# Order of the scale total, two conversions and six loads at the head of the joint down projection

## The chip, the cores and the metric

The kernel runs on one core of a Trainium2 chip. The metric is device time in microseconds (us). The core has a matrix engine (TensorE, "PE" in the profile; its weight loads are "PEld"), three engines for elementwise work (VectorE "DVE", ScalarE "ACT", GpSimd "POOL") and SyncE ("SP"), which in this kernel issues most DMA transfers. Each engine takes its own list of instructions in order; engines wait for each other by semaphores.

## The reference

One transformer block on a sequence of 2048 rows of 1024 values, bf16 in and out: a layer norm and a sliding, dilated attention with an output product (`wo`), added to the input; then a second layer norm and a gated bilinear feed-forward, also added:

```python
g = jnp.einsum("bsd,df->bsf", x, w_gate)      # 1024 -> 3584
u = jnp.einsum("bsd,df->bsf", x, w_up)
h = g * u
return jnp.einsum("bsf,fd->bsd", h, w_down)   # 3584 -> 1024
```

The change lies in the last product, the down projection, for the first two of four chunks of 512 rows.

## The kernel before

The rows are worked in four chunks of 512. Attention is elementwise work on DVE; projections are 128x512 matmuls on PE. The order of the work is written by hand, engine by engine: what is recorded first on an engine runs first on it. The attention of a chunk is a generator, and `pull(n)` records its next n steps at the place where it stands; around the change a step of chunk 3's attention is one DVE instruction on 128x4096 values (L523, L532 or L534, 2.3 us each).

**The joint down projection.** The gated rows h of chunks 0 and 1 are multiplied with `w_down` together, as a 2x2 block product with seven instead of eight block products. A1x are gated rows of chunk 0, A2x of chunk 1 (x: 1 for even, 2 for odd blocks of 128 inner values); B11, B21 are the left 512 columns of `w_down` for even and odd blocks, B12, B22 the right ones. Chunk 0's gated rows stay in on-chip memory. Chunk 1's were written to the DRAM tensor `hd1` (L752) and are loaded back as `a21` and `a22` (`load_h1`, L973 to L979), each in two parts: 8 blocks and 6 blocks. `b12` is loaded by `load_down` (L927) into two tiles. All of these loads are issued by SP.

Where sums of blocks are formed, the operands are converted to f16 in place, with a power of two as scale: `scale_h1` for h, `scale_d` for `w_down`. A scale comes from a sum of absolute values: ACT adds up pieces of the matrix into columns of `l1d` (L635), `rows()` reduces the columns to one value for each partition and casts it to bf16 (DVE, L639 and L640), `total()` adds over the partitions with one matmul with ones on PE (L645) and turns the total into the scale and its inverse with five small DVE instructions (L647 to L654).

The work around the change, in the order in which it is written:

1. `wo_adds(2, ...)`: the `wo` product of chunk 2 on PE, its sums on DVE (L1000), some attention steps between them, and on ACT the absolute sums of B11 and B21 (`abs_blocks`, the last columns that `scale_d` needs).
2. The loop of L1069: four products A11 x B11 into `ex0` to `ex3`, 14 matmuls each (`dprod`, L944). Between them, by `q`, stand the conversions of `a21` and `a22` (`conv_h1`; part 0 on DVE, L925, part 1 on ACT, L923), the half sums S1 = a21 + a22 (`s1_half`, DVE, L1042), `scale_d.rows()` and, after the third product, `scale_d.total()` into the bank of `ey3`.
3. `seed` (ACT, L1067) copies each `ex` times `scale_d` to `ey`; then ACT multiplies `ey` by the scale of h (L1089).
4. A12 x B21 on top of the same `ex` (L1098). Its first matmul overwrites `ex0`, so it waits for `seed(0)`. On DVE beside it: `put` (L784, the finished left half of chunk 0's result), conversions of `b11` and `b12` (L925), and the differences T1 = b12 - b11 in two halves (`t_half`, L937).
5. S1 x T1 into `ev` (L1116), 56 matmuls. The first needs S1 and the first half of T1, the eighth the second half of T1. Then `ey` takes two more products (L1132 and following). On ACT from step 3 on: the conversions of chunk 0's rows (L1095, 14 of 128x512), of `b22` (L1096), and of A12 (L1104).

The tiles of `b22` lie where a22's two parts lay, so their loads wait for the two half sums. `b22`'s loads are the next that SP issues after the six loads above.

Of the kernel before, what the change touches and what calls it, by code (L numbers as in the profile page):

```python
# [78 lines left out]
def kernel(  # L79
# [11 lines left out]
    nc = tc.nc  # L91
# [565 lines left out]
    scale_gu, scale_d, scale_h = Scale("gu", 28), Scale("d", 23), Scale("h", 56)  # L657
# [260 lines left out]
    def f16(ap):  # L918
        return ap.bitcast(F16)

    def to_f16(dst, src, sc, eng=nc.vector):
        if eng is nc.scalar:
            nc.scalar.activation(dst, src, ACTF.Copy, scale=sc)  # L923
        else:
            eng.tensor_scalar(dst, src, sc, None, ALU.mult)  # L925

    def load_down(homes, e, hf):  # L927
        for a, t in enumerate(homes):
            nc.sync.dma_start(t[:, 0:NH, :], wd_e[e][:, bass.ts(a, NH), bass.ts(hf, 512)])
# [12 lines left out]
    def dprod(ps, q, lhs, rhs, fresh, lo=0, n=TC):  # L942
        for k in range(NP):
            nc.tensor.matmul(ps[:, bass.ds(lo, n)], lhsT=lhs[k][:, bass.ts(q, 128)], rhs=rhs[k][:, bass.ds(lo, n)],  # L944
                             start=(fresh and k == 0), stop=(k == NP - 1), skip_group_check=not fresh)
# [13 lines left out]
    def pull(n):  # L959
        for _ in range(n):  # L960
            next(atts[3], None)
# [3 lines left out]
    def halves(parts, name):  # L965
        return [pool.tile([128, KO, TC], BF, tag=tag, name=f"{name}{i}") for i, (pool, tag) in enumerate(parts)]

    b12 = halves(((att, "qD"), (att, "kD")), "b12")
    load_down(b12, 0, 1)
    a21 = halves(((lnTp, "lnT"), (lnTp, "lnT")), "a21")  # L970
    a22 = halves(((lnTp, "lnT"), (wpool, "w")), "a22")

    def load_h1(dst, e, parts=(0, 1)):  # L973
        for i in parts:
            t, k, n = ((dst[0], 0, 8), (dst[1], 8, 6))[i]
            nc.sync.dma_start(t[:, 0:n, :], hd1[:, 2 * k + e:2 * (k + n):2, :])

    load_h1(a21, 0)
    load_h1(a22, 1)  # L979
    state["live"] += 1  # L980

    def cells_of(homes, n=8):
        return [t[:, k, :] for t in homes for k in range(n)][0:NP]
# [55 lines left out]
    def s1_half(i):  # L1039
        n = (8, 6)[i]  # L1040
        s, t = (f16(a[i][:, 0:n, :]) for a in (a21, a22))
        nc.vector.tensor_tensor(s, s, t, ALU.add)  # L1042

    def conv_h1(a, i, eng=nc.vector):
        n = (8, 6)[i]
        to_f16(f16(a[i][:, 0:n, :]), a[i][:, 0:n, :], scale_h1.s, eng)
# [19 lines left out]
    def seed(q):  # L1066
        nc.scalar.activation(ys[q][:], xs[q][:], ACTF.Copy, scale=scale_d.s)  # L1067

    for q in range(4):  # L1069
        dprod(xs[q], q, A11, cells_of(b11, NH), True)  # L1070
        if q == 0:
            conv_h1(a21, 0)
            conv_h1(a22, 0)
            s1_half(0)
            scale_d.rows()
        if q == 1:
            pull(1)
            conv_h1(a21, 1, nc.scalar)
            conv_h1(a22, 1, nc.scalar)
        if q == 2:  # L1080
            scale_d.total(ys[3])
            inv1 = const.tile([128, 1], F32, name="inv_h1d")
            nc.vector.tensor_tensor(inv1[:], scale_h1.inv, scale_d.inv, ALU.mult)
            inv1 = inv1[:]
            for i in range(3):
                seed(i)
    seed(3)
    for q in range(4):
        nc.scalar.activation(ys[q][:], ys[q][:], ACTF.Copy, scale=scale_h1.s)  # L1089
    pull(1)  # L1090
    s1_half(1)
    b22 = halves(((lnTp, "lnT"), (wpool, "w")), "b22")
# [48 lines left out]
    a22 = halves(((att, "vD"), (att, "oD")), "a22r")  # L1141
# [212 lines left out]
```

## Time and profile before

| what | value |
|---|---|
| median of 4 runs | 773.78 us (773.57 to 775.03) |
| the profiled execution | 773.83 us, of which its span, from first to last instruction, is 772.0 us |
| PE busy | 760.2 us, 98% of the span |
| DVE busy | 606.0 us, 78% |
| ACT busy | 513.3 us, 66% |
| POOL busy | 142.1 us, 18% |
| from 412 to 428 us: PE, DVE, ACT busy | 13.37, 14.10, 13.49 of 16 us |
| from 428 to 440 us: PE, DVE, ACT busy | 11.92, 11.80, 12.00 of 12 us |
| granted TensorE clock | 1.000 |

How to read it: a matmul of 128x512 is listed with 379 ns, but matmuls are pipelined, and a new one starts about every 0.216 us; so PE counts as busy for 98% of the span, and what stands still on it is best seen as a gap between starts. In a row of the timeline the numbers ahead are the start in the span and the duration; brackets at the end hold how long the engine had been idle before and what ended that. Instructions of one kind in a row are merged (x14).

### The profile page before, as it was taken

The numbers are of one execution on the slowest core, as the hardware profiler recorded it, in microseconds if no ns is written. First come the engines' busy times: TensorE is split into PE (matmuls) and PEld (weight loads), VectorE is DVE, ScalarE is ACT, GpSimd is POOL, SyncE is SP. The second block draws the span as 40 slices with busy tenths as digits, with TensorE's granted clock in tenths as the row PEclk, the third lists the DMA queues.
The fourth block names the chain that finished last, engine by engine and source line by source line (L and its number), as shares of the span: only waits on it lengthen the run. The fifth ranks groups of instructions, "written<-read, shape, count | busy, mean of one in ns | idle before, by whom it ended". The sixth has DMA issues, their size and how long they took to land.

```text
span 772.0 us, 10243 instructions
## 1 busy us (share of the span) xinstructions
PE 760.2 (98%) x3607; PEld 350.6 (45%) x3663; DVE 606.0 (78%) x718; ACT 513.3 (66%) x979; POOL 142.1 (18%) x152
## 2 busy tenths in 40 slices
PE   8999999999999999999998999999999999999998
PEld 5444444444444444444443444444444444444444
DVE  5629999999999999999999996985553444568863
ACT  4648966423687398778899985836677677788240
POOL 0000000200002000020000001008778687600000
PEclk9999999999999999999999999999999999999999
DMA  7999796999966799479568457674332423740001
GB/s 267 268 256 258 206 273 153 271 312 284 306 206 215 225 293 300 155 263 314 186 202 281 125 189 241 141 178 106 99 102 62 110 63 102 243 139 28 0 28 54
DMA packets 190915, 144.85 MB, mean 188 GB/s; under 512 B 81808, under 2 KB 181136, under 8 KB 188688
## 3 DMA queue, kind: packets, MB, share of 16 engines
q1 hardware_dynamic: 180416, 116.94, 54.0%
q0 software_dynamic: 3584, 22.02, 8.4%
q10 hardware_dynamic: 6864, 5.24, 2.5%
q8 instruction: 28, 0.46, 0.3%
q14 instruction: 23, 0.19, 0.1%
HBM read 110.10 MB, written 27.26 MB: 178 GB/s over the span
## 4 chain that ended last, share of the span: by engine, by line
PE 73%; DVE 16%; ACT 4%; DMA 4%; issue 3%; ACTq 0%; SPq 0%; DVEq 0%
PE ps L431 19%; PE dx L944 6%; PE pz L826 6%; PE py L826 6%; PE px L826 6%; PE pg L431 4%; PE pu L431 4%; PE pv L826 3%; PE ez L944 3%; PE ey L944 3%; DVE pv L523 3%; PE dy L944 3%; DVE prod L477 2%; PE wo L602 2%; PE wo L998 2%
## 5 line engine op out<-in xcount | busy, mean ns | idle before, releaser
L431 PE MATMUL ps<-lnT,w_qkv 128*128 128x512 bf16 x720 | 158.8, 379 | 1.2 <-DMA lnT<-ln 0.4
L431 PEld LDWEIGHTS <-w_qkv 128*128 128x128 bf16 x736 | 71.8, 98 | 86.8 <-issue 0.9
L344 ACT CAST sg<-ps 128x512 bf16<-128x512 f32 x96 | 55.2, 586 | 47.4 <-PE ps L431 38.5
L477 DVE TENSOR_TENSOR prod<-qD,kD 128x4096 bf16<-128x4096 bf16 x32 | 72.2, 2284 | 12.7 <-DMA kD<-kd 12.6
L523 DVE TENSOR_TENSOR pv<-vD,at 128x4096 bf16<-128x4096 bf16 x32 | 72.4, 2285 | 0.2
L826 PEld LDWEIGHTS <-sw 128*128 128x128 f16 x448 | 43.8, 98 | 52.9 <-issue 0.2
L431 PEld LDWEIGHTS <-w_wu 128*128 128x128 bf16 x448 | 43.9, 98 | 52.8
L431 PEld LDWEIGHTS <-w_wg 128*128 128x128 bf16 x448 | 43.8, 98 | 52.9
L826 PE MATMUL px<-lnT,ws 128*128 128x512 bf16 x212 | 53.1, 379 | 0.6
L536 POOL DMA_DIRECT2D od<-oD x4 | 2.2, 542 | 275.6 <-DVE oD L534 275.6
L431 PE MATMUL pwu<-lnT,w_wu 128*128 128x512 bf16 x219 | 52.5, 379 | 0.3
L431 PE MATMUL pwg<-lnT,w_wg 128*128 128x512 bf16 x220 | 52.5, 379 | 0.2
L431 PE MATMUL pg<-lnT,w_wg 128*128 128x512 bf16 x222 | 52.6, 379 | 0.1
L431 PE MATMUL pu<-lnT,w_wu 128*128 128x512 bf16 x218 | 52.4, 379 | 0.3
L826 PEld LDWEIGHTS <-ws 128*128 128x128 f16 x336 | 32.9, 98 | 39.7
L807 POOL TENSOR_TENSOR sw<-ws 128x512 f16<-128x512 f16 x26 | 30.0, 1152 | 85.6 <-PE pv L826 51.9
L944 PEld LDWEIGHTS <-gs 128*128 128x128 f16 (+1 forms) x280 | 27.4, 98 | 36.0 <-issue 3.2
L479 DVE TENSOR_TENSOR prod<-prod 128x4096 bf16<-128x4096 bf16 x16 | 36.6, 2289 | 0.4
L843 ACT COPY py<-px 128x512 f32<-128x512 f32 x28 | 16.0, 570 | 27.5 <-PE px L826 27.5
L808 POOL TENSOR_TENSOR sw<-sw,ws 128x512 f16<-128x512 f16 x26 | 30.0, 1154 | 2.0
L809 POOL TENSOR_TENSOR sw<-ws 128x512 f16<-128x512 f16 x26 | 30.0, 1153 | 0.0
L810 POOL TENSOR_TENSOR sw<-ws,sw 128x512 f16<-128x512 f16 x26 | 30.0, 1153 | 0.0
(334 smaller groups left out, 1471.9 us busy)
## 6 DMA issues: line engine op xcount, KB each, us to landing
w_wg<-in_B_w_gate_dram SPq DMA_DIRECT2D x14, 1024.0 KB, 7.0
w_wu<-in_B_w_up_dram SPq DMA_DIRECT2D x14, 1024.0 KB, 6.4
w_pair<-in_B_w_gate_dram SPq DMA_DIRECT2D x14, 512.0 KB, 4.0
w_pair<-in_B_w_up_dram SPq DMA_DIRECT2D x14, 512.0 KB, 5.3
w_wo<-in_A_wo_dram SPq DMA_DIRECT2D x6, 1024.0 KB, 7.9
w_qkv<-in_A_wqkv_dram SPq DMA_DIRECT2D x5, 1024.0 KB, 11.4
kd<-sg SPq DMA_DIRECT2D x32, 144.0 KB, 4.5
kD<-kd POOLq DMA_DIRECT2D x4, 1152.0 KB, 8.7
```

Of the source, the lines that this page charges most:

```text
L344: nc.scalar.copy(sg[:, HB:HB + TC], ps[:])
L431: nc.tensor.matmul(ps[:], lhsT=wt[:, ko, bass.ts(j, 128)], rhs=rhs[:, ko, :], start=(ko == 0), stop=(ko == KO - 1))
L477: nc.vector.tensor_tensor(prod[:, j], qD[:], kD[:, :, o:o + SUB], ALU.mult)
L479: nc.vector.tensor_tensor(prod[:, :, 0:16], prod[:, :, 0:16], prod[:, :, 16:32], ALU.add)
L523: nc.vector.tensor_tensor(pv[:, j], vD[:, :, o:o + SUB], at[:, w, None, :].to_broadcast((128, DH, SUB)), ALU.mult)
L807: eng.tensor_tensor(sw[:, i, 0], a21, a22, ALU.add)
L808: eng.tensor_tensor(sw[:, i, 1], sw[:, i, 0], a11, ALU.subtract)
L809: eng.tensor_tensor(sw[:, i, 2], a11, a21, ALU.subtract)
L810: eng.tensor_tensor(sw[:, i, 3], a12, sw[:, i, 1], ALU.subtract)
L826: nc.tensor.matmul(ps[:], lhsT=lhs[:, ko, :], rhs=rhs[:, ko, :], start=(fresh and ko == 0), stop=(ko == 3), skip_group_check=not fresh)
L843: nc.scalar.copy(yb[i][:], xb[i][:])
L944: nc.tensor.matmul(ps[:, bass.ds(lo, n)], lhsT=lhs[k][:, bass.ts(q, 128)], rhs=rhs[k][:, bass.ds(lo, n)], start=(fresh and k == 0), stop=( ...
```

## The change

Three things move; no instruction is added or taken away. The loads of `a21` and `a22` are issued ahead of those of `b12`. `scale_d.rows()` stands between the two DVE conversions instead of after the first half sum. Behind `scale_d.total()` now come, on DVE, the first half sum and one attention step, which stood ahead of it; and on ACT the conversion of a22's second part comes after the seeds and the four scalings, where it had come before the seeds.

```diff
@@ -966,7 +966,6 @@
     b12 = halves(((att, "qD"), (att, "kD")), "b12")
-    load_down(b12, 0, 1)
     a21 = halves(((lnTp, "lnT"), (lnTp, "lnT")), "a21")
     a22 = halves(((lnTp, "lnT"), (wpool, "w")), "a22")
@@ -977,6 +976,7 @@
     load_h1(a21, 0)
     load_h1(a22, 1)
+    load_down(b12, 0, 1)
     state["live"] += 1
@@ -1070,23 +1070,23 @@
         dprod(xs[q], q, A11, cells_of(b11, NH), True)
         if q == 0:
             conv_h1(a21, 0)
+            scale_d.rows()
             conv_h1(a22, 0)
-            s1_half(0)
-            scale_d.rows()
         if q == 1:
-            pull(1)
             conv_h1(a21, 1, nc.scalar)
-            conv_h1(a22, 1, nc.scalar)
         if q == 2:
             scale_d.total(ys[3])
             inv1 = const.tile([128, 1], F32, name="inv_h1d")
             nc.vector.tensor_tensor(inv1[:], scale_h1.inv, scale_d.inv, ALU.mult)
             inv1 = inv1[:]
+            s1_half(0)
+            pull(1)
             for i in range(3):
                 seed(i)
     seed(3)
     for q in range(4):
         nc.scalar.activation(ys[q][:], ys[q][:], ACTF.Copy, scale=scale_h1.s)
+    conv_h1(a22, 1, nc.scalar)
     pull(1)
     s1_half(1)
     b22 = halves(((lnTp, "lnT"), (wpool, "w")), "b22")
```

## The prediction

> **What bounds the kernel now.** I read the page's first part, then the waits of PE, then the timeline from 396 to 452 us, engine by engine.
>
> ```profile
> PE 760.2 (98%) x3607; PEld 350.6 (45%) x3663; DVE 606.0 (78%) x718; ACT 513.3 (66%) x979; POOL 142.1 (18%) x152
> ```
>
> PE is the bound over the whole span, so the change can only gain where PE stands still near it. The waits of PE (total, times, longest) show where:
>
> ```profile
> PE ey L645 <- DVE rowbd L640: 2.4, 1, 2.4
> ...
> PE ex L944 <- ACT ey L1067: 0.2, 1, 0.2
> ```
>
> The matmul of `scale_d.total()` is PE's longest wait anywhere. The timeline of the place:
>
> ```profile
> 412.80 9.23 PE L944 MATMUL ex<-w_dn,gs 128*128 128x512 bf16 x41
> ...
> 419.02 0.19 ACT L635 ACTIVATION_READ_ACCUMULATOR junkb<-w_dn 128x1 f32 x1
> 419.12 2.84 ACT L923 ACTIVATE a<-a,sbh 128x3072 f16<-128x3072 bf16 x1
> 420.50 1.28 DVE L925 TENSOR_SCALAR a<-a,sbh 128x4096 f16<-128x4096 bf16 x1 [1.69 <-DMA a<-hd]
> ...
> 421.82 2.29 DVE L1042 TENSOR_TENSOR a<-a,a 128x4096 f16<-128x4096 f16 x1
> ...
> 424.44 0.38 PE L645 MATMUL ey<-rowbd,ones 128*128 128x512 bf16 x1 [2.42 <-DVE rowbd L640]
> ...
> 427.32 2.40 ACT L1067 ACTIVATE ey<-ex,sbd 128x512 f32<-128x512 f32 x4 [1.79 <-DVE ibd L654]
> ...
> 428.03 12.25 PE L944 MATMUL ex<-w_dn,gs 128*128 128x512 bf16 x55 [0.19 <-ACT ey L1067]
> ...
> 429.60 1.75 DVE L1042 TENSOR_TENSOR a<-a,a 128x3072 f16<-128x3072 f16 x1
> ...
> 431.26 0.68 DVE L784 SCALAR_TENSOR_TENSOR h<-ex,h 128x512 bf16<-128x512 f32 x1
> ...
> 434.27 0.69 DVE L784 SCALAR_TENSOR_TENSOR h<-ex,h 128x512 bf16<-128x512 f32 x1 [0.20 <-PE ex L944]
> ...
> 437.00 2.02 DVE L937 TENSOR_TENSOR w_dn<-b,w_dn 128x3584 f16<-128x3584 f16 x1
> ...
> 439.54 2.01 DVE L937 TENSOR_TENSOR w_dn<-b,w_dn 128x3584 f16<-128x3584 f16 x1
> ...
> 440.11 12.25 PE L944 MATMUL ev<-w_dn,a 128*128 128x512 f16 x56
> ```
>
> The reader is to see two things. First the stall: DVE waits for a DMA until 420.50, so the half sum and `rows()` are late and PE waits. Second, what comes after: the second half of T1 ends at 439.54 + 2.01 = 441.55, and the eighth `ev` matmul, which needs it, is due at 440.11 + 7 x 0.216 = 441.62. DVE is 0.07 us ahead of PE there. So PE can start `ev` earlier only if DVE finishes T1 earlier.
>
> **The change part by part.** A matmul's slot is (452.20 - 440.11) / 56 = 0.216 us, from the starts of `ev` and of `ey` after it.
>
> *PE's stall goes.* The absolute sums on ACT end at 419.02 + 0.19 = 419.21. DVE has by then converted a21's first part (start 417.53, next start about 1.2 us on) and runs the reduce and the cast (0.38 us by their rows): the row sums stand at 419.6. PE's 42 matmuls from 412.80 end at 412.80 + 42 x 0.216 = 421.87; the total starts there, not at 424.44, without a wait. The fourth `ex` product starts at 422.09 and A12 x B21 could start 14 slots later, at 425.11.
>
> *The total's tail.* The matmul ends at 421.87 + 0.38 = 422.25. DVE's hand-off from PE costs 0.03 us (ex1's last matmul ends at 434.24, `put` starts at 434.27), so the copy starts at 422.28. Before, copy to first seed took 427.32 - 426.51 = 0.81: seeds start at 423.09. DVE meanwhile has nothing to do from about 420.9 to 422.28: it was behind PE before, and now it waits for PE. Nothing is gained on DVE by the earlier conversion.
>
> *DVE, by itself.* The tail with inv1 takes 427.39 - 426.51 = 0.88, to 423.16. Then the half sum (421.82 to 424.03: 2.21), L534 (2.20) and L523 (429.60 - 427.39 = 2.21): the second half sum could start at 429.78, against 429.60 before.
>
> *ACT, where the conversion was moved.* The seeds and scalings take 0.572 each (2.29 for four). Three seeds run from 423.09 to 424.81. The fourth needs the fourth product, whose last matmul ends at 422.09 + 13 x 0.216 + 0.38 = 425.28; it runs from 425.31 to 425.88, the four scalings to 428.17, and the conversion of a22's second part (2.85 by two rows) to 431.02. Before, it was done at 425.52. Queued behind it on ACT are the 14 conversions of L1095, which start at 431.0 instead of 431.89, so nobody there is late. But the second half sum on DVE waits for it: from 429.78 to 431.05, 1.27 us of a wait which was not there. Behind that wait on DVE stand `put`, four conversions and both halves of T1.
>
> *T1 and PE.* The half sum takes 431.26 - 429.60 = 1.66, so the first `put` starts at 432.71, 1.45 later than before. The second `put` no longer waits for PE: before, it could have started at 432.93 + 1.06 = 433.99 and started at 434.27. That gives 0.28 back. Both halves of T1 are therefore 1.17 later: the second ends at 442.72. PE reaches the end of A12 x B21 at 425.11 + 56 x 0.216 = 437.2, waits about 3.0 us for the first half of T1 (439.02 + 1.17 = 440.19), runs seven matmuls and waits again, about 1.0 us, until 442.75. The other 49 matmuls end at 453.33, against 452.20: **1.1 us later than before**. PE's stall of 2.57 + 0.35 us (425.11 against 428.03) is not gone; it is moved behind A12 x B21 and made longer.
>
> *After it.* From 452.2 to 490 PE is busy 37.70 of 37.8 us and from 490 to 515 24.98 of 25, so there is no idle time in which the 1.1 us could vanish; I pass it to the end. DVE's next work for PE (the sums of L1112, then t2) ended at 450.7 for matmuls due from 452.2 on; both move by the same 1.1, so the spare 1.5 us stays.
>
> *The loads.* SP issues the six loads between 403.49 and 414.6 and then nothing until 424.14, so no other entry is passed. The four `a` loads now have 1.84 MB less ahead of them, 5.3 us at the 349 GB/s of that stretch. Bounds for a22's first part: no gain at all (420.48) or the whole 5.3 us (415.2). At the late end its conversion finishes at 421.8, still ahead of the copy at 422.28; a22's second part (422.6 at the latest) is wanted at 428.17. `b12` lands with the last bytes, about 422.7, and is wanted at 434.1. So the reorder is worth nothing, covered on the one side by DVE's wait for PE's total and on the other by 11 us. Without the cover it would cost DVE what the data is late.
>
> *b22.* Its two loads wait for the half sums and move from 424.14 to about 425.4 and from 431.4 to 432.8. They took 4.9 to 7.1 us, so the second lands by 439.9 at the latest; ACT wants the tiles at 439.6 and 442.8. Behind them SP issues the results' stores and chunk 3's rows, not wanted before the next `wo` at 476. Nothing.
>
> **Bounds of what the trace doesn't show.** The wait of the second half sum for ACT is new. At the low end ACT is done in time and DVE alone decides: the first `put` at 429.78 + 1.66 = 431.44, less 0.28, shift -0.1 us, time 773.7. At the high end the PE to DVE and DVE to ACT hand-offs cost 0.2 us more each than the 0.03 and 0.10 of their rows, and the shift is 1.5. I take 1.1, because each term of it has a row of the same instruction. The other unknown is how PE runs after standing still for 3.0 us; the longest wait in the trace is 2.42, and the granted clock stays 1.00 from 421 to 425 around it. The nearest row of a slow PE is the start of the kernel:
>
> ```profile
> 1.20 4.28 PE L338 MATMUL warm_ps<-warm 128*128 128x512 bf16 x13 [1.20 <-DVE warm L324]
> ```
>
> Thirteen matmuls at full pace take 12 x 0.216 + 0.38 = 2.97 us; these took 4.28. So a slow restart costs between nothing and 1.3 us; I take nothing, by the 2.42 us row.
>
> [...]
>
> **Sum.** The profiled execution took 773.83 us, 0.05 over the median of 773.78: 773.83 + 1.13 = 774.96, say 775.0.
>
> **The rivals.**
>
> *The stall is simply gone: 770.9.* PE keeps 2.92 us if nothing else holds `ev`. For it: the wait for L640 is PE's longest, and it does go. Against: T1 would have to be done 2.9 us earlier, and its DVE chain is the same work without gaps, starting from a copy that PE allows at 422.28.
>
> *DVE does not wait for ACT: 773.7.* The low end above. It needs the moved conversion done by 429.78, 1.2 us ahead of my sum; the fourth seed, which PE releases, speaks against it.
>
> *The gap behind A12 x B21 slows PE: 776.3.* One mechanism: while PE waits about 3.0 us for the first half of T1, its clock drops, and the 1.3 us of the start's row are added to my 1.1. It decides from some length between 2.42 us, which did no harm, and what the new gap turns out to be.
>
> **How the numbers follow.** My forecast (ACT's conversion holds DVE, DVE holds `ev`) gets 0.74. The DVE-only case gets 0.10, the slow restart 0.11, the full gain 0.05. About what a measurement of this kernel can tell from no change is 0.2%, 1.55 us: above 775.4 counts as slower, below 772.3 as faster. Of my forecast's 0.74 I put 0.13 above 775.4, since the high end of the shift touches it; so slower gets 0.11 + 0.13 = 0.24, faster 0.05, within 0.71. The range from 773.6 to 776.4 takes in the low end of the shift, the forecast and the slow restart, and leaves out the full gain.
>
> **What would show it.** The wait of PE at L645 is gone and the total starts near 421.9. The second half sum has an idle time of about 1.3 us ahead of it, ended by ACT L923. The first `ev` matmul shows a wait for DVE L937 of about 2.9 us, a second follows seven matmuls later, and `ey` starts near 453.3. I am wrong if `ev` starts before 440, if the half sum waits for a DMA, or if matmuls after the gap run at a longer slot.

## The result, and the profile after

The changed kernel takes 775.2 us in the median of 41 runs (774.39 to 777.48), the kernel before 774.6 us in 61 runs taken beside it (773.39 to 776.86). The ratio is 1.001, with a 95% interval of 1.0006 to 1.0015: 0.5 to 1.2 us slower. The profiled execution took 775.12 us, with a span of 773.3 us and a mean granted clock of 0.998.

The waits of PE in the changed kernel (total, times, longest): the wait for the row sums (L640) is gone, and one of 2.9 us stands ahead of `ev`.

```profile
PE ev L944 <- DVE w_dn L937: 2.9, 1, 2.9
PE warm_ps L338 <- DVE warm L324: 1.2, 1, 1.2
```

The timeline of the changed kernel, the rows that answer to those of before:

```profile
412.26 9.23 PE L944 MATMUL ex<-w_dn,gs 128*128 128x512 bf16 x41
...
421.33 0.38 PE L645 MATMUL ey<-rowbd,ones 128*128 128x512 bf16 x1
...
421.74 0.16 DVE L647 COPY totd<-ey 128x1 f32<-128x1 f32 x1 [1.46 <-PE ey L645]
...
422.56 1.82 ACT L1067 ACTIVATE ey<-ex,sbd 128x512 f32<-128x512 f32 x3 [1.14 <-DVE ibd L654]
...
427.63 2.88 ACT L923 ACTIVATE a<-a,sbh 128x3072 f16<-128x3072 bf16 x1
...
430.54 1.76 DVE L1042 TENSOR_TENSOR a<-a,a 128x3072 f16<-128x3072 f16 x1 [1.09 <-ACT a L923]
...
437.66 2.02 DVE L937 TENSOR_TENSOR w_dn<-b,w_dn 128x3584 f16<-128x3584 f16 x1
...
439.73 13.93 PE L944 MATMUL ev<-w_dn,a 128*128 128x512 f16 x56 [2.92 <-DVE w_dn L937]
...
440.20 2.01 DVE L937 TENSOR_TENSOR w_dn<-b,w_dn 128x3584 f16<-128x3584 f16 x1
...
453.50 6.85 PE L944 MATMUL ey<-t,gs 128*128 128x512 f16 x31
```

The total's matmul no longer waits, DVE now waits 1.46 us for it, ACT converts a22's second part from 427.63, the second half sum waits 1.09 us for that, T1's halves end at 439.68 and 442.21, and `ev` starts with the first. The 56 `ev` matmuls then take 453.50 - 439.73 = 13.77 us, where before took 12.09. The busy times by stretch of the changed kernel (busy us and counts of PE, PEld, DVE, ACT, POOL, then the granted clock, the DMA share and GB/s) show why:

```profile
430.00:437.00 7.00, 6.81 (x32) 2.98 (x31) 6.46 (x7) 7.00 (x12) 0.00 (x0) 1.00 0.45 154
437.00:440.50 3.50, 0.77 (x3) 0.32 (x3) 3.50 (x4) 3.50 (x5) 0.00 (x0) 0.95 0.09 30
440.50:443.00 2.50, 2.50 (x7) 0.91 (x6) 2.50 (x3) 2.50 (x2) 0.00 (x0) 0.50 0.20 59
443.00:447.00 4.00, 4.00 (x18) 1.73 (x17) 4.00 (x13) 4.00 (x4) 0.00 (x0) 0.93 0.72 227
```

PE is "busy" for all of 440.5 to 443, but with 7 matmuls where 12 fit at 0.216 us each: the granted clock is 0.50.

### The profile page after: what moved, and what is told of

Read it like the earlier page. It is cut to its first block, busy times and chain, and to the rows that moved or that the text cites. A ratio compares the mean times of both kernels' runs of the same rounds, so it can differ in the third digit from the quotient of the medians.

```text
span 773.3 us, 10245 instructions
## 1 busy us (share of the span) xinstructions
PE 762.8 (99%) x3607; PEld 351.4 (45%) x3663; DVE 606.3 (78%) x718; ACT 513.1 (66%) x979; POOL 142.0 (18%) x152
## 4 chain that ended last, share of the span: by engine, by line
PE 95%; DVE 3%; ACT 1%; issue 1%; DVEq 0%
PE ps L431 20%; PE dx L944 6%; PE pz L826 6%; PE pg L431 6%; PE py L826 6%; PE pwg L431 6%; PE pwu L431 6%; PE pu L431 6%; PE px L826 6%; PE wo L998 4%; PE pv L826 3%; PE ez L944 3%; PE ey L944 3%; PE dy L944 3%; PE ev L944 2%; PE wo L602 2%
## 5 line engine op out<-in xcount | busy, mean ns | idle before, releaser
L431 PE MATMUL ps<-lnT,w_qkv 128*128 128x512 bf16 x720 | 158.7, 379 | 0.8
L431 PEld LDWEIGHTS <-w_qkv 128*128 128x128 bf16 x736 | 71.8, 98 | 86.2 <-issue 0.3
L431 PEld LDWEIGHTS <-w_wg 128*128 128x128 bf16 x448 | 43.9, 98 | 52.8
L431 PEld LDWEIGHTS <-w_wu 128*128 128x128 bf16 x448 | 43.8, 98 | 52.9
L431 PE MATMUL pg<-lnT,w_wg 128*128 128x512 bf16 x222 | 52.6, 379 | 0.1
L431 PE MATMUL pu<-lnT,w_wu 128*128 128x512 bf16 x218 | 52.4, 379 | 0.3
L431 PE MATMUL pwg<-lnT,w_wg 128*128 128x512 bf16 x220 | 52.5, 379 | 0.2
L431 PE MATMUL pwu<-lnT,w_wu 128*128 128x512 bf16 x219 | 52.5, 379 | 0.3
```

Of the source, the lines that this page charges most:

```text
L431: nc.tensor.matmul(ps[:], lhsT=wt[:, ko, bass.ts(j, 128)], rhs=rhs[:, ko, :], start=(ko == 0), stop=(ko == KO - 1))
```

## The experiments

Theory A: `ev` starts when T1 is done; T1 is the end of a chain on DVE which in the kernel before starts with the arrival of a22, and in the changed kernel is held by ACT's conversion of a22's second part; behind PE's wait of 2.92 us the clock drops to 0.50. The rivals stand with each run. Ratios are to the kernel before, run beside on the same chip.

**1. ACT's conversion back ahead of the seeds** (the changed kernel, this part undone):

```diff
             conv_h1(a21, 1, nc.scalar)
+            conv_h1(a22, 1, nc.scalar)
...
-    conv_h1(a22, 1, nc.scalar)
     pull(1)
```

> The changed kernel with one part undone: ACT converts a22's second part before the seeds again. Theory A (the moved conversion holds the second half sum, and through it T1 and ev): the conversion ends at about 424.8, the first seed a little later than in the changed kernel (about 424.8 against 423.1), A12 x B21 starts at about 425.5; the second half sum starts when DVE is free, about 429.8, without a wait for ACT; ev starts at about 439.0 after a gap of some 1.4 us, at full clock; time about 773.7 to 773.9, that is 0.1 to 0.2 below before's undisturbed profile (773.83), 1.1 to 1.4 below the changed kernel. Rival B (only the slow clock behind the gap costs anything, and the place of the conversion does not matter): the gap stays near 2.9 us, and the time stays at about 775.

Measured: 773.5 us, ratio 0.9987 (0.9979 to 0.9996). DVE's wait for the total, its second half sum and PE in its timeline:

```profile
421.79 0.16 DVE L647 COPY totd<-ey 128x1 f32<-128x1 f32 x1 [1.46 <-PE ey L645]
...
429.41 1.75 DVE L1042 TENSOR_TENSOR a<-a,a 128x3072 f16<-128x3072 f16 x1
```

```profile
438.60 1.67 PE L944 MATMUL ev<-w_dn,a 128*128 128x512 f16 x7 [1.55 <-DVE w_dn L937]
441.13 10.73 PE L944 MATMUL ev<-w_dn,a 128*128 128x512 f16 x49 [0.86 <-DVE w_dn L937]
```

The half sum starts without a wait, 1.1 us earlier, and so does `ev`, which now shows both waits, one for each half of T1. From the first `ex` matmul to `ey` PE takes 39.39 us, as in before's profile (39.40): PE's old stall has moved, not gone. All 11 executions kept the full clock. Rival B is out: the conversion's place is worth 1.15 us between executions at full clock (spans of 772.75 and 771.6), and the clock the smaller rest of the 1.7 us between the medians.

**2. The loads alone** (the kernel before, with the loads of `a21` and `a22` first):

```diff
-    load_down(b12, 0, 1)
...
     load_h1(a22, 1)
+    load_down(b12, 0, 1)
```

> The kernel before with one part of the change alone: the loads of a21 and a22 ahead of those of b12. Theory A (DVE's chain from a22's arrival to T1 sets ev): DVE's wait of 1.7 us for the load goes, the row sums stand at about 422.6 instead of 424.4, the total's matmul starts at about 422.7, the seeds at about 425.6, A12 x B21 at about 426.3, T1's second half ends at about 439.8, and ev starts at about 438.3 instead of 440.11: 1.8 us less than before, about 772.1. Rival C (what the prediction said of the reorder: it is worth nothing): 773.8. Rival D (the store of the last gated rows holds the first a loads and delays b12 behind them): slower than 774.5.

Measured: 771.82 us, ratio 0.9967 (0.9955 to 0.9979), 5 executions. DVE and PE in its timeline:

```profile
416.81 2.47 DVE L925 TENSOR_SCALAR a<-a,sbh 128x4096 f16<-128x4096 bf16 x2
419.32 2.29 DVE L1042 TENSOR_TENSOR a<-a,a 128x4096 f16<-128x4096 f16 x1
```

```profile
421.94 0.38 PE L645 MATMUL ey<-rowbd,ones 128*128 128x512 bf16 x1 [0.64 <-DVE rowbd L640]
...
437.61 12.25 PE L944 MATMUL ev<-w_dn,a 128*128 128x512 f16 x56
```

This one part, alone, gains what the whole change loses and more. DVE goes from the first conversion to the second without a wait, the first half sum, the seeds and T1 come 2.5 us earlier in the span, PE's wait falls from 2.42 to 0.64, and `ev` follows A12 x B21 without one. C and D are out: the reorder has a value, which the other moves hide. Experiment 1 shows where the first part of it goes. It has the early loads too, with the row sums early and the first half sum and an attention step behind the total, and its median span at full clock is 1.9 us longer (771.6 against 769.7): there DVE stands still 1.46 us for the total's matmul, where here it works on the half sum and an attention step.

**3. Filling the gap** (the changed kernel, with 11 matmuls in it):

```diff
+        for _ in range(11 if q == 0 else 0):
+            nc.tensor.matmul(ev[:], lhsT=ones[:], rhs=scale_d.rowb[:].to_broadcast((128, TC)), start=True, stop=True)
         dprod(ev, q, FS1, fcells(b11), True)
```

> The changed kernel with 11 additional matmuls of ones times the row sums into the bank of ev0, between A12 x B21 and ev, whose results are overwritten; they fill about 2.4 us of the gap of 2.9 us. Theory A (ev's start is set by T1, and the clock drops in the gap): ev's first matmul starts where it did, about 439.7, but at full clock; it now waits again before the eighth, until T1's second half at 442.2, and the next product starts at about 452.9 instead of 453.5: 0.6 to 0.7 us less than the changed kernel in executions where its clock dropped, about 774.4. Rival B (only the clock costs anything): the time falls to that of before or below, 773.8 or less. Rival E (additional matmuls only push ev back): 775 or more.

Measured: 774.54 us, ratio 1.0 (0.9991 to 1.0008), all 12 executions at a clock of 1.0. PE in its timeline:

```profile
436.65 2.56 PE L1117 MATMUL ev<-rowbd,ones 128*128 128x512 bf16 x11
439.73 1.67 PE L944 MATMUL ev<-w_dn,a 128*128 128x512 f16 x7 [0.52 <-DVE w_dn L937]
442.26 10.74 PE L944 MATMUL ev<-w_dn,a 128*128 128x512 f16 x49 [0.86 <-DVE w_dn L937]
452.84 7.50 PE L944 MATMUL ey<-t,gs 128*128 128x512 f16 x34
```

`ev` starts at 439.73, to the digit as in the changed kernel, since T1 does. At full clock it waits again for the second half, and `ey` starts 0.66 earlier (452.84 against 453.50). So the clock costs the changed kernel 0.66 us and not 1.68: its slow matmuls ran where PE would have waited. B and E are out.

**4. Two attention steps behind T1 and t2** (the kernel of experiment 1, with them moved; the five steps are these two, the two that stood there and one more, which had stood among the later sums):

```diff
             s1_half(0)
-            pull(1)
             for i in range(3):
...
-    pull(1)
     s1_half(1)
...
-    pull(2)
+    pull(5)
     retire(4)
```

> The changed kernel with ACT's conversion of a22's second part ahead of the seeds and with the two attention steps of chunk 3 (4.4 us of DVE) behind T1, F11's sums and t2, where now five steps stand instead of two. Theory A (T1's chain on DVE is the bound): the second half sum starts at about 425.4, the puts follow PE (about 428.7, 431.7), T1's halves end at about 436.4 and 439.0, A12 x B21 starts at about 425.5 and ends at 437.6, and ev starts there without a wait: 2.5 us less than before, about 771.3, if the later attention output does not hold chunk 3's wo product (its transposed load lands at about 472 and the product starts at about 473.9). Rival F (that load is late): ev starts as said, but wo waits, and the time is 772 to 774.

Measured: 770.61 us, ratio 0.9953 (0.9941 to 0.9965), 5 executions, the fastest of all, faster than both kernels. DVE and PE:

```profile
428.01 0.69 DVE L784 SCALAR_TENSOR_TENSOR h<-ex,h 128x512 bf16<-128x512 f32 x1 [1.38 <-PE ex L944]
```

```profile
436.88 12.25 PE L944 MATMUL ev<-w_dn,a 128*128 128x512 f16 x56
```

The first `put` waits for PE now, not PE for DVE; from the first `ex` matmul (412.30) to `ey` (448.96) PE has no wait. `wo` starts at 473.1 without one, so F did not come true.

**5. Filling the wait of the kernel before** (11 matmuls ahead of the total's):

```diff
+            for _ in range(11):
+                nc.tensor.matmul(ys[3][:], lhsT=ones[:], rhs=scale_h1.rowb[:].to_broadcast((128, TC)), start=True, stop=True)
             scale_d.total(ys[3])
```

> The kernel before with 11 additional matmuls of ones times the row sums of h into the bank of ey3 ahead of the total's matmul, which overwrites them; they fill 2.4 of the 2.6 us in which PE stands still there. The repeats of the kernel before fall into two groups, spans near 771.9 us at a granted clock of 0.999 to 1.000 and near 773.2 at 0.997 to 0.998. Theory A (the clock drops in that wait in about half of the executions): all executions at 0.999 or more, spans of 771.6 to 772.2, time about 773.7, and its median about 0.9 below that of the kernel before. Rival G (the two groups come from elsewhere, or from the chip): the two groups stay.

Measured: 773.52 us, ratio 0.999 (0.9981 to 0.9999), all 11 executions at full clock, spans 771.4 to 772.1. PE and DVE in its timeline:

```profile
421.35 2.56 PE L1082 MATMUL ey<-rowbh,ones 128*128 128x512 bf16 x11
424.44 0.38 PE L645 MATMUL ey<-rowbd,ones 128*128 128x512 bf16 x1 [0.54 <-DVE rowbd L640]
```

```profile
420.50 1.29 DVE L925 TENSOR_SCALAR a<-a,sbh 128x4096 f16<-128x4096 bf16 x1 [2.20 <-DMA a<-hd]
```

So matmuls of no use made the kernel before faster by 0.1%, though the total starts at 424.44 as before: with its wait of 2.42 us unfilled, the clock drops in many executions. In those run beside experiments 1 to 8, 28 of 50 lie at a clock of 0.997 or 0.998, with a median span near 773.1, and the other 22 at 0.999 or 1.0, with 771.9. Rival G is out. That the drop stands in this wait is shown by filling it; no profile of before caught one.

**6. Loads and attention steps, without the early row sums** (experiment 2 with the steps moved as in 4).

> The loads of a21 and a22 first and the two attention steps behind t2, but the row sums still behind the first half sum and ACT's conversion ahead of the seeds. Theory A: the total's matmul still waits 0.6 us for the row sums; the seeds no longer wait for an attention step, so A12 x B21 follows the fourth product without a wait, ev follows A12 x B21; 0.35 below the run with the loads alone and 0.6 above the run that had the row sums early too: about 771.2. Rival H (the place of the row sums is worth nothing once the loads come early): 770.6, as that run.

Measured: 771.12 us, ratio 0.9957 (0.9945 to 0.997), 5 executions. PE in its timeline:

```profile
422.11 0.38 PE L645 MATMUL ey<-rowbd,ones 128*128 128x512 bf16 x1 [0.64 <-DVE rowbd L640]
```

The total waits 0.64 us for the row sums, and that is the only wait from `ex` to `ey`. Beside experiment 4 (770.61) the early row sums, with the half sum behind the total, are worth about 0.5 us. Rival H is out; the two medians were taken in different groups of runs, but their spans (769.1 to 769.4 against 768.5 to 768.8) do not overlap, and before's median span at full clock is 771.9 in both groups.

**7. The attention steps moved, the conversion left late** (the changed kernel, with the steps moved as in 4).

> The changed kernel with only the two attention steps moved behind t2; ACT's conversion of a22's second part stays behind the seeds. Theory A (ACT's conversion holds the second half sum and so T1): taking 4.4 us of work off DVE ahead of it changes nothing, the half sum starts at about 430.5 after 5.5 us or so of idle time ended by ACT, ev starts at about 439.7 with a wait of 2.9, time 774.5 to 775.3, as the changed kernel. Rival I (the amount of work on DVE sets T1): 772 or less.

Measured: 775.09 us, ratio 1.0005 (0.9996 to 1.0014). DVE and PE:

```profile
430.81 1.76 DVE L1042 TENSOR_TENSOR a<-a,a 128x3072 f16<-128x3072 f16 x1 [5.61 <-ACT a L923]
```

```profile
440.01 13.91 PE L944 MATMUL ev<-w_dn,a 128*128 128x512 f16 x56 [2.92 <-DVE w_dn L937]
```

With 4.4 us less on DVE nothing moves: DVE's wait for ACT grows from 1.09 to 5.61 and PE's stays at 2.92. Rival I is out. The same edit with the conversion ahead of the seeds is experiment 4, 4.5 us faster (3.9 between executions at full clock).

**8. The row sums alone** (the kernel before):

```diff
             conv_h1(a21, 0)
+            scale_d.rows()
             conv_h1(a22, 0)
             s1_half(0)
-            scale_d.rows()
```

> The kernel before with one part of the change alone: the row sums between the two conversions. Theory A: the total's matmul starts near 421.9 without a wait, but the attention step and the late half sum stand ahead of the copy of the total on DVE, so the seeds start at about 427.0 and A12 x B21 at about 427.7, with the wait now between the fourth product and it; T1 ends 0.3 earlier, and the time in an execution at full clock is 773.5, with some executions about 1.3 longer, since PE stands still for more than 2 us. Rival J (the wait for the row sums is the loss): PE's 2.4 us are saved, 771.4.

Measured: 774.14 us, ratio 0.9997 (0.9988 to 1.0006). PE in its timeline:

```profile
427.66 12.25 PE L944 MATMUL ex<-w_dn,gs 128*128 128x512 bf16 x55 [2.93 <-ACT ey L1067]
```

PE's wait for the row sums is gone and stands, 2.93 us long, behind the fourth product, where A12 x B21 waits for the first seed. Seven of 11 executions at full clock have a median of 773.8, the four at 0.997 or 0.998 one of 775.4. Rival J is out: taking that wait away, by itself, gained nothing.

## Why the prediction was right, and where it was wrong

The forecast was 775.0, no change that can be told at 0.2%; measured are 775.2 and a ratio of 1.001.

- *PE's stall goes and comes back behind A12 x B21, longer.* Right. Set against the first `ex` matmul (0.54 us earlier than in before's profile), the forecast of 421.87 for the total came at 421.87, of 423.09 for the seeds at 423.10, of 431.05 for the second half sum at 431.08, of 442.72 for T1's end at 442.75, and of 440.2 for `ev` at 440.27.
- *ACT's moved conversion holds DVE.* Right, shown by experiments 1 and 7. The wait was 1.18 from start to start (430.54 - 427.16 - 2.20; 1.27 forecast).
- *The loads are worth nothing.* For the whole change this was argued, and no run has the changed kernel without the reorder. Rows of experiment 8, which has the early row sums and the late loads, speak for it: its second conversion starts at 420.40, when the data is there, and DVE goes on at 421.72, next to the 421.74 of the copy in the changed kernel. Alone, the early loads are worth 2.0 us against before's executions at full clock (773.8) and 2.8 against its median (experiment 2). The step said why they were covered, but not that the cover is made by the other moves.
- *PE after the gap: "I take nothing, by the 2.42 us row".* Wrong. In 30 of 42 executions of the changed kernel the mean clock is 0.998 or less, and in the profiled one the clock was 0.50 behind the gap. The row of one execution was no bound: in 28 of 50 others, with the same wait in the program, the mean clock is 0.997 or 0.998, and with the wait filled in none of 11 (experiment 5). The price was also mis-sized: 1.3 us were added to the shift, but the slow matmuls overlap the second wait, and 0.66 is left.
- *The 1.1 us are passed to the end.* The mechanism was right, the size off. From the first `ex` matmul to `ey` the profile of before took 39.40 us and the changed kernel at full clock (experiment 3) 40.58: 1.18. But in before's profile PE reached this stage at 412.80, where the other profiles have it at 412.08 to 412.54; one wait of 0.4 us ahead of it (L431 for a transposed load) stands only there. The kernel before hides such lateness, since its chain waits for a load: in experiment 5 PE is there at 412.29, and DVE's second conversion starts at 420.50 and `ey` at 452.20 all the same. The changed chain follows PE. So where PE is on time, `ey` comes 0.64 us later than before's (452.84 against 452.20), and full-clock spans differ by 0.85 (772.75 of 12 executions against 771.9 of 22). The 0.2 us between these two was not traced.
- *The sum against the median.* The median of before that the forecast starts from is of 4 executions; over 61 it is 774.6. The kernel before pays the clock too, about 1.2 us in 28 of 50 executions, the changed one about 0.75 in 30 of 42. By these shares, 0.85 + 0.71 x 0.75 - 0.56 x 1.2 = 0.7 us, which is what the medians (0.6) and the ratio (0.8) show, against 1.1 forecast. That the time itself came out within 0.2 us is partly luck: the shift at full clock was 0.3 us too large in the forecast, and the changed kernel's clock, 0.5 us in the mean, was left out.
- *The signs.* The total started without a wait, DVE stood idle ahead of the second half sum until ACT L923 was done (1.09), and `ev` waited 2.92 us for L937. Of the signs of being wrong one came true in full, the longer slot behind the gap, and it is the step named above. `ev` did start before 440, at 439.73, because the whole stage came 0.54 earlier. The second wait, seven matmuls later, is not in the changed kernel's profile, where slow matmuls fill it; at full clock it is there (0.86, experiment 3).
- *The rivals.* The full gain of 2.9 us did not come; experiment 4 shows the price was about right, with T1 moved too. The DVE-only case is experiment 1, forecast 773.7, measured 773.5. The slow matmuls behind the gap came (0.40 to 0.43 us apart), at half the price: 0.66 us against 1.3.

## What to carry to other kernels

When an engine's wait is taken away, ask what its next instructions wait for and follow that chain back on every engine: here two engines were 0.07 us apart, and taking the wait away only moved it. Try the parts of a change one by one. Here the early loads alone gained about 0.3% and the early row sums alone nothing. With both, and with the half sum and an attention step behind the total, most of the gain was gone (experiment 1), since DVE stood still for the total instead of working ahead; no run separates the early row sums from the half sum's new place there. The late conversion took the rest and more, because it stands behind work that waits for the engine it was to feed. Work that is due later (two attention steps) is worth moving behind the chain that is due now, but only once nothing else holds that chain.

## What the runs showed of the hardware

In the kernels where PE stands still for 2.4 to 2.9 us in this stage, the granted clock dropped in a part of the executions. The mean clock of an execution is 0.998 or less in 28 of 50 executions of the kernel before (a wait of 2.42 us in its profile), 30 of 42 of the changed kernel (2.92), 6 of 11 in experiment 7 (2.92) and 4 of 11 in experiment 8 (2.93); in none of 49 executions of the kernels whose longest wait here is 1.55 us or less (experiments 1 to 6). Two profiles caught a drop, those of the changed kernel and of experiment 7, and both show 0.50: in the changed kernel the clock is at 0.50 from 440.18 to 443.59, and nine matmuls behind the gap start 0.40 to 0.43 us apart, over 3.4 us in all. In before's profile the clock stays at 1.00 around its wait of 2.42 us, and experiment 8's profile, with one of 2.93, has a mean clock of 1.0.

What in an execution sets whether it drops was not tested.
